# One order replaced by another: h of batches 6 and 7 in 512-token pieces, loads in halves, first q by two queues

## The chip, the cores and the metric

The kernel runs on one core of a Trainium2 chip. The metric is device time in microseconds of one execution, the median of several runs. The engines that matter are PE (TensorE, matmuls and transposes), DVE (VectorE), ACT (ScalarE), POOL (GpSimd, which here issues the casting loads), SP (SyncE, which issues the other transfers) and the core's 16 DMA engines. PE writes to eight PSUM banks, which DVE and ACT empty.

## The reference

```python
def _attn_ref(q, k, v, g_norm) -> np.ndarray:
    kv = np.einsum('bhsd,bhse->bhde', k, v)
    out = np.einsum('bhsd,bhde->bhse', q, kv)
    rms = np.sqrt(np.mean(out * out, axis=-1, keepdims=True) + 1e-06)
    return (out / rms * g_norm).astype(np.float32)

def _moe_ref(x, w_in, conv_w, w_out) -> np.ndarray:
    h = np.maximum(x @ w_in, 0.0)
    ...
    for k in range(K):
        conv_out += conv_w[k][None, None, :] * hp[:, k:k + S, :]
    gate = 1.0 / (1.0 + np.exp(-conv_out))
    return (h * gate @ w_out).astype(np.float32)
```

q, k and v are float32 of (batch 8, heads 8, tokens 576, 64). The attention has no softmax: k and v of a head make a 64 x 64 matrix, q goes through it, and each head's row is normed. The heads of a token then make a row x of 512, and a feed-forward part follows: h of 1024 columns, a convolution over three neighbouring tokens of each column, a sigmoid gate, and the way back to 512.

## The kernel before

Nothing in this kernel is scheduled by a loop. The string `ORDER` lists 773 steps, each a token such as `kv.4.1@0` (step, batch 4, pair of head pairs 1, in PSUM bank 0) or `rea.1.3.0!V` (the engine that does it, V for DVE and A for ACT). A loop at the end of the kernel body runs the step's function for each token, and each engine, SP and POOL too, executes what its steps issue in exactly that order. A step late on an engine makes all behind it on that engine late. The numbers after `@` are slots: a PSUM bank or a buffer, so a step also waits until whoever used that slot last is done with it.

The steps that the change and the prediction speak of:

- `pre` loads q, k and v of head pairs 0 and 1 of batch 0, and all of k, by SyncE as float32 into a staging tile (`stg`, `stg2`; two of four head-pair tiles make one transfer of 576 KB). `ca.x.w` casts one tile of it to bf16, on DVE or ACT.
- `Lq.b.u`, `Lk.b.u`, `Lv.b.u` load half u of a batch by POOL's queue, cast to bf16 on the way (288 KB written). Without u (`Lq.7`) it is the whole batch. q, k and v each have two buffers, so a load waits for the last reader of the batch that had its buffer before. `Li.j` and `Lo.i` load the weights.
- `qt`, `qc` transpose q and copy it from PSUM; `kv`, `kvc` make and copy the 64 x 64 matrices; `ot` multiplies.
- Batches 0 and 1: `sq`, `on`, `nl`, `mz` square, sum, take the reciprocal root and write x. Batches 2 to 7, in the groups of `NORM`: `sq`, `oc` (copy of the output), `ss`, `ln`, `sl`, `sp`, `mu`. x of a batch is complete with its last `mz` or `mu`.
- h of a batch alone: `hm.b.f.u` (two halves u of the contraction, each four matmuls of 288 columns) and `re`, the ReLU that empties it, 576 columns. h of a pair of batches, 1152 columns, for the pairs in `PAIRH`: `ha.p.f.e` (512 columns, e = 0 or 1, four matmuls) and `rea`, and `hb.p.j` (the last 128 columns for four f at once) and `reb`.
- The convolution c (`CONV`: 0 and 1 are batches 0 and 1, 2 is batches 2 and 3 together, 3 is 4 and 5, and 4 and 5 are batches 6 and 7): `ta`, `aa`, `ab` on DVE, the sigmoid `sg` on ACT, and the gate's product `mg` on DVE. One set of 24 DVE steps of each kind, whatever the order.
- `om.p.k.i.j` is the product with w_out for 128 tokens, `ea` copies it to a row buffer, `st` stores it by SyncE. The last tokens, `om.3.6`, are done in two halves of 256 columns.
- `fi`, `fq` and `fo` are fillers, matmuls on a zero tile. They compute nothing. `fi.36.128` is 36 matmuls of 128 columns.
- `sw.k.6` makes the next store wait until the named load has landed.
- `NoSync` dependencies at the end of the kernel body fix each engine's order.

The constants: `HALF` lists the batches whose loads go in halves, `PAIRH` the pairs whose h is made for both batches at once, `STORES2` the stores that go row block by row block.

Of the kernel before, what the change touches and what calls it, by code (L numbers as in the profile page):

```python
# [66 lines left out]
STORES2 = [(0, 0), (0, 3), (0, 2), (0, 1)]  # L67
# [4 lines left out]
pre@0,0,0 Lq.0.1 ca.q.0!V ca.q.1!V fi.36.128@0 fi.3.128@0 qt.0.0@0 qc.0.0!V@0 fi.1.512@2 fi.20.128@2 ct@0 ca.k.1!V  # L72
ca.k.0!A pn Lv.0.1 ca.v.0!V Lq.1.1@1 ca.v.1!A fq.1.512.0@1 fq.1.256.0@1 kv.0.0@1 Li.2 kvc.0.0!A pc fq.2.512.3@3
ot.0.0@6,4 ca.k.2!A sq.0.0@0 Li.0 fi.3.512@1 fi.2.128@1 on.0.0@0 nl.0.0@0 ca.k.3!V fq.2.512.0@2 fq.1.256.0@2 qt.0.1@2
qc.0.1!V@0 sq.0.1@0 mz.0.0@0 fi.1.512@0 fi.3.128@0 on.0.1@0 nl.0.1 fo.1.384.0.1 kv.0.1@2 kvc.0.1!V Lq.1.0 Li.3
fo.1.384.0.1 fq.1.256.1@6 ot.0.1@6,0 sq.0.2@0 mz.0.1 fq.1.512.0@2 qt.1.1@2 Li.1 Lv.1.0@1 fi.2.128@4 on.0.2@4 sq.0.3@7
nl.0.2@0 qc.1.1!V@0 fo.2.384.0.2 on.0.3@2 nl.0.3 Lk.1.0@1 fo.1.384.0.3 hm.0.5.0@4 mz.0.2 Lq.2.0@0 hm.0.4.0@2 mz.0.3
hm.0.1.0@6 hm.0.5.1 re.0.5!A@0 hm.0.4.1 ta.0.5@0 hm.0.1.1 re.0.4!A ta.0.4 qt.1.0@0 hm.0.0.0@2 hm.0.0.1 hm.0.3.0@4
hm.0.3.1 re.0.1!A ta.0.1@1 Lv.1.1 hm.0.6.0@6 qc.1.0!A@1 Lv.2.1@0 re.0.0!A aa.0.2 hm.0.2.0@0 hm.0.2.1 ab.0.2
fq.1.512.0@2 kv.1.0@2 sg.0.4 ta.0.0 re.0.3!V aa.0.0 Lk.1.1 sg.0.5 ab.0.0 kvc.1.0!A hm.0.6.1 re.0.2!A ot.1.0@4,2  # L80
hm.0.7.0@0 mg.0.2 re.0.6!V sg.0.0 Lq.3.1@1 sq.1.1@0 Lq.2.1 hm.0.7.1 ta.0.3@0 re.0.7!V ta.0.2 qt.2.0@6 qc.2.0!V@1
sq.1.0@1 aa.0.1 fo.5.384.1.1 on.1.0@0 sg.0.1 mg.0.0 nl.1.0@0 fo.5.384.1.0 on.1.1@6 nl.1.1 fo.2.384.1.0 kv.1.1@0
kvc.1.1!A fo.1.384.1.1 fq.1.256.2@6 ot.1.1@0,6 mz.1.0 mz.1.1 sq.1.2@0 qt.3.1@4 sq.1.3@1 Lk.2.1@0 qc.3.1!V@0 Lv.2.0
ab.0.1 on.1.2@2 nl.1.2@0 fo.2.384.1.2 on.1.3@4 nl.1.3 Lk.2.0 mz.1.2 fo.1.384.1.3 hm.1.7.0@2 qt.2.1@4 mz.1.3 hm.1.5.0@0
ta.0.6@1 sg.0.2 ta.0.7 hm.1.7.1 hm.1.5.1 sg.0.3 qc.2.1!V@2 re.1.7!A hm.1.1.0@6 hm.1.1.1 hm.1.4.0@4 Lv.3.1@1 re.1.1!A
hm.1.4.1 aa.0.3 mg.0.1 re.1.5!A kv.2.0@6 re.1.4!A Lo.0 hm.1.2.0@0 hm.1.2.1 ab.0.3 sg.0.6 sg.0.7 hm.1.6.0@2 ta.1.5@0
ta.1.4 Lk.3.1@1 kvc.2.0!V hm.1.6.1 Lo.1 ot.2.0@4,6 re.1.2!A re.1.6!A Lq.3.0 oc.2.1@0 kv.2.1@0 kvc.2.1!A Lq.5.0@0
hm.1.3.0@2 aa.1.2 mg.0.3 hm.1.3.1 sq.2.1@0 hm.1.0.0@0 hm.1.0.1 ta.1.7@1 sq.2.0@1 oc.2.0 ab.1.2 sg.1.5 om.0.0.0.0@7
sg.1.4 re.1.3!V ta.1.6 re.1.0!V ot.2.1@5,3 oc.2.3@1 sq.2.3@2 Lq.5.1 kv.3.1@0 om.0.0.0.1@2 aa.1.3 mg.1.2 om.0.0.1.1
Lk.3.0 sq.2.2@3 oc.2.2 kvc.3.1!V ot.3.1@0,3 ta.1.0@0 Lv.3.0 ea.0.0.1!A@0 ab.1.3 ta.1.1 qt.3.0@5 sg.1.7 sg.1.6  # L90
qc.3.0!V@0 oc.3.3@2 aa.1.0 mg.1.3 sq.3.3@4 om.0.1.1.0@2 oc.3.2 ta.1.3@1 om.0.1.0.0 ea.0.1.0!A@1 Lk.5.1@0 Lq.4.1@1
ta.1.2 om.0.1.0.1@6 om.0.0.1.0 ab.1.0 sq.3.2@5 ea.0.0.0!A aa.1.1 ab.1.1 om.0.1.1.1 sg.1.0 qt.5.1@0 qt.5.0@2 kv.3.0@4
qc.5.1!V@1 sg.1.1 ea.0.1.1!V qc.5.0!V@2 kvc.3.0!A Lq.4.0 om.0.2.1.1@7 mg.1.0 sg.1.3 sg.1.2 ot.3.0@0,4 om.0.2.1.0@6
sq.3.1@6 om.0.3.1.1@2 Lv.5.1@0 sq.3.0@7 ss.2@3 ss.3 ln.1@0 mg.1.1 oc.3.1@3 oc.3.0 sl.1@0 om.0.2.0.1 om.0.3.0.1 st.0.0
ea.0.3.1!A@2 kv.5.1@4 qt.4.1@0 Lk.5.0 sp.3.1.1@2 kvc.5.1!V Lk.4.1@1 mu.3.1.1@0 sp.2.0.1@4 mu.2.0.1 om.0.2.0.0
qc.4.1!A@0 sp.3.0.0@0 sp.3.1.0@2 ea.0.2.1!A@0 om.0.3.1.0@7 sp.3.0.1@4 mu.3.0.0 Lv.5.0 sp.2.1.1@0 mu.3.1.0 om.0.3.0.0
mu.3.0.1 sp.2.1.0@2 ea.0.2.0!A sp.2.0.0@4 mu.2.1.1 mu.2.0.0 mu.2.1.0 hb.1.0@6 Lv.4.1@1 fq.1.256.0@0 kv.4.1@0
ea.0.3.0!A kv.5.0@4 reb.1.0!A@1 kvc.5.0!V ot.5.1@6,2 kvc.4.1!A sq.5.2@0 oc.5.2@0 sq.5.3@1 ha.1.3.0@0 rea.1.3.0!V
ha.1.3.1@1 rea.1.3.1!V oc.5.3 ta.2.3@0 Lk.4.0 ot.5.0@6,4 ha.1.2.0@0 Lv.4.0 rea.1.2.0!V ha.1.2.1@3 oc.5.0@1 rea.1.2.1!V
ta.2.2 sq.5.1@2 Lk.7@0 oc.5.1 aa.2.1 ha.1.1.1@1 kv.4.0@4 sq.5.0@3 rea.1.1.1!A ot.4.1@6,2 kvc.4.0!A qt.4.0@0 oc.4.2@2  # L100
sq.4.3@4 qc.4.0!V@0 ab.2.1 oc.4.3 sq.4.2@5 ha.1.1.0@4 rea.1.1.0!A ta.2.1@1 ha.1.0.0@5 rea.1.0.0!A ha.1.0.1@2
ot.4.0@0,3 rea.1.0.1!A ta.2.0 aa.2.0 sq.4.1@6 sq.4.0@7 ha.1.6.0@5 ha.1.5.1@2 ss.4@6 oc.4.1@3 oc.4.0 ss.5 rea.1.5.1!A
ln.2@0 Lq.7@0 qt.7.1@3 qc.7.1!A@0 qt.7.0@0 om.0.4.0@2 sl.2@0 om.0.4.1 ab.2.0 ha.1.5.0@3 Lv.7@0 rea.1.6.0!A sp.5.0.1@4
sp.5.1.1@6 mu.5.0.1@1 qc.7.0!A@1 Lv.6@1 ea.0.4!A@3 sp.4.1.1@0 mu.4.1.1 ha.1.4.0@2 rea.1.5.0!A sg.2.0 hb.1.1@3 Lq.6@1
mu.5.1.1 sp.5.1.0@0 rea.1.4.0!V sp.5.0.0@4 kv.7@6 ha.1.4.1@2 reb.1.1!A kvc.7!A sp.4.0.0@6 mu.5.0.0 mu.5.1.0 sg.2.1
rea.1.4.1!A sp.4.1.0@4 mu.4.0.0 sp.4.0.1@0 mu.4.1.0 ha.1.7.1@3 sg.2.3 mu.4.0.1 sw.q.6 st.0.4 hb.2.1@2 reb.2.1!V@0
sg.2.2 ot.7.0@4,6 mg.2.0 Lk.6@1 ta.2.5@1 rea.1.7.1!A oc.7.1@0 ta.2.4 kv.6@0 ha.1.7.0@2 kvc.6!V sq.7.1@0 ha.2.3.0@3
# [31 lines left out]
def kernel(  # L139
# [11 lines left out]
    nc = tc.nc  # L151
# [18 lines left out]
    T = {}  # L170
# [87 lines left out]
    def pre():  # L258
# [3 lines left out]
        for x in "qkv":  # L262
            nc.sync.dma_start(out=T["stg"][:, "qkv".index(x)], in_=rows(x, 0, 0, 2))
        if FIRST:
# [4 lines left out]
            out=cw_rows[NR - 1:NR, :].rearrange("o (i d) -> o i d", i=2),  # L269
# [440 lines left out]
```

## Time and profile before

| | |
|---|---|
| median of 3 runs (lowest, highest) | 179.21 us (179.1, 179.8) |
| profiled execution | 179.12 us, span 177.3 us |
| PE busy | 170.3 us, 96% of the span |
| DVE busy | 157.0 us, 89% |
| ACT busy | 139.7 us, 79% |
| POOL busy | 34.7 us, 20% |
| DMA | 27.22 MB, 153 GB/s mean |

The span is the time on the core from the first to the last instruction; the profiled execution's own time has 1.8 us around it. Matmuls are pipelined, so one that is shown as 379 ns long may start 216 ns after the one before; the spacing, not the length, adds up. The profile's chain of waits goes back from the last instruction, at each step to what released it.

The profile has DMA rates in 40 equal slices of 4.43 us:

```profile
DMA  5999999999999996999881000005710000043594
GB/s 184 366 201 200 202 206 210 202 206 208 206 207 233 230 206 88 207 210 205 183 301 64 0 2 4 0 3 213 272 49 0 0 0 4 0 172 123 218 379 173
```

The DMA engines are busy from 4.4 us to 66 us without a break. The casting loads read twice the bytes that they write; the rate counts what is written. The issues by kind, with the size of one and the median time from issue to landing in us:

```profile
q_sb<-in_q_dram POOLq DMA_DIRECT2D x11, 288.0 KB, 10.6
v_sb<-in_v_dram POOLq DMA_DIRECT2D x11, 288.0 KB, 10.7
k_sb<-in_k_dram POOLq DMA_DIRECT2D x10, 288.0 KB, 10.8
stg<-in_k_dram SPq DMA_DIRECT2D x2, 576.0 KB, 6.0
stg<-in_q_dram SPq DMA_DIRECT2D x1, 576.0 KB, 3.9
stg<-in_v_dram SPq DMA_DIRECT2D x1, 576.0 KB, 6.3
```

### The profile page before, as it was taken

To read this page: it belongs to the slowest core of one execution; us is meant where nothing else is said; L and a number is where in the kernel's file an instruction comes from. 1 tells how busy PE (TensorE), PEld (TensorE's weight loads), DVE (VectorE), ACT (ScalarE), POOL (GpSimd) and SP (SyncE) were. 2 spreads that over 40 slices of the span, in tenths; PEclk is the share of its full clock that TensorE was granted. 3 is DMA by queue.
4 is the path that set the end of the run, shared out by engine and by line. 5 is a ranking of instruction groups with operands and counts; after the bars stand their busy time and mean duration, and the time that the engine had idled before them with its cause. 6 is when DMAs were issued, how large, how long until landed. Compare 5 with 4: busy or idle time off the path is not lost.

```text
span 177.3 us, 5289 instructions
## 1 busy us (share of the span) xinstructions
PE 170.3 (96%) x2253; PEld 95.4 (54%) x2253; DVE 157.0 (89%) x282; ACT 139.7 (79%) x219; POOL 34.7 (20%) x60
## 2 busy tenths in 40 slices
PE   7999998899999999999999999999999999999992
PEld 7755765576444454444554454444577754444451
DVE  2757699999999796999999999999999999999931
ACT  2366799899999938999999999987795966494720
POOL 6945640851067005500000000000000000000000
PEclk9999999999999999999999999999999999999999
DMA  5999999999999996999881000005710000043594
GB/s 184 366 201 200 202 206 210 202 206 208 206 207 233 230 206 88 207 210 205 183 301 64 0 2 4 0 3 213 272 49 0 0 0 4 0 172 123 218 379 173
DMA packets 21355, 27.22 MB, mean 153 GB/s; under 512 B 1224, under 2 KB 15828, under 8 KB 21332
## 3 DMA queue, kind: packets, MB, share of 16 engines
q0 software_dynamic: 15072, 15.09, 51.5%
q1 hardware_dynamic: 6256, 11.80, 18.0%
q8 instruction: 17, 0.28, 0.6%
q14 instruction: 6, 0.05, 0.1%
q10 hardware_dynamic: 4, 0.00, 0.0%
HBM read 32.52 MB, written 9.44 MB: 237 GB/s over the span
## 4 chain that ended last, share of the span: by engine, by line
PE 66%; DVE 14%; DMA 8%; ACT 7%; issue 2%; POOL 1%; ACTq 0%; DVEq 0%
PE banks L628 28%; PE banks L534 13%; PE banks L547 12%; DMA v_sb<-in_v_dram 6%; PE banks L296 3%; PE banks L441 2%; ACT sq L448 2%; PE banks L393 2%; ACT h L238 2%; DVE xT L518 2%; DMA out_dram<-row 2%; PE banks L418 2%; DVE taps L583 2%; DVE taps L596 2%; DVE taps L584 1%
## 5 line engine op out<-in xcount | busy, mean ns | idle before, releaser
L628 PE MATMUL banks<-w_out_sb,h 128*128 128x512 bf16 x280 | 63.7, 379 | 0.2
L603 ACT ACTIVATE taps<-taps,cw 128x576 bf16<-128x576 bf16 (+1 forms) x48 | 43.6, 946 | 9.9 <-DVE taps L596 9.8
L628 PEld LDWEIGHTS <-h 128*128 128x128 bf16 x280 | 26.5, 98 | 31.5 <-issue 1.6
L238 ACT ACTIVATE h<-banks 128x512 bf16<-128x512 f32 (+1 forms) x51 | 29.8, 658 | 5.7 <-PE banks L534 4.2
L534 PE MATMUL banks<-xT,w_in_sb 128*128 128x288 bf16 x256 | 33.5, 286 | 0.4
L547 PE MATMUL banks<-xT,w_in_sb 128*128 128x512 bf16 x128 | 30.1, 379 | 0.2 <-ACT row L232 0.2
L534 PEld LDWEIGHTS <-w_in_sb 128*128 128x128 bf16 x256 | 24.6, 98 | 8.3 <-issue 1.6
L232 ACT ACTIVATE row<-banks 128x512 f32<-128x512 f32 (+1 forms) x29 | 16.8, 601 | 9.6 <-PE banks L628 5.6
L590 DVE TENSOR_TENSOR taps<-taps 128x1152 bf16<-128x1152 bf16 (+1 forms) x24 | 22.9, 956 | 0.5
L596 DVE TENSOR_TENSOR taps<-taps,h 128x1152 bf16<-128x1152 bf16 (+1 forms) x24 | 22.8, 952 | 0.3
L609 DVE TENSOR_TENSOR h<-h,taps 128x1152 bf16<-128x1152 bf16 (+1 forms) x24 | 22.7, 951 | 0.2 <-ACT taps L603 0.2
L583 DVE TENSOR_SCALAR taps<-h,cw 128x576 bf16<-128x576 bf16 (+1 forms) x48 | 20.3, 423 | 1.7 <-ACT h L238 1.5
L448 ACT ACTIVATE sq<-banks 128x576 bf16<-128x576 f32 x32 | 20.4, 674 | 1.7 <-PE banks L441 1.7
L584 DVE TENSOR_SCALAR taps<-h,cw 128x576 bf16<-128x576 bf16 (+1 forms) x48 | 20.1, 418 | 0.0
L547 PEld LDWEIGHTS <-w_in_sb 128*128 128x128 bf16 x128 | 11.8, 98 | 14.4 <-issue 1.3
L518 DVE SCALAR_TENSOR_TENSOR xT<-o,cw,banks 128x576 bf16<-128x576 f32 x24 | 18.1, 806 | 0.4 <-PE banks L511 0.3
L232 ACT ACTIVATE o<-banks 128x576 f32<-128x576 f32 x24 | 15.9, 678 | 0.0
L240 DVE TENSOR_SCALAR h<-banks 128x576 bf16<-128x576 f32 (+1 forms) x17 | 12.2, 720 | 1.1 <-PE banks L547 1.0
L354 POOL DMA_DIRECT2D k_sb<-in_k_dram x12 | 8.7, 726 | 20.0 <-PE banks L441 9.4
L227 ACT ACT_TABLE_LOAD x8 | 10.3, 1283 | 2.1 <-issue 2.0
L354 POOL DMA_DIRECT2D v_sb<-in_v_dram x13 | 9.4, 724 | 11.2 <-PE banks L324 4.7
L354 POOL DMA_DIRECT2D q_sb<-in_q_dram x13 | 9.6, 738 | 7.5 <-PE banks L418 6.5
(74 smaller groups left out, 149.1 us busy)
## 6 DMA issues: line engine op xcount, KB each, us to landing
out_dram<-row SPq DMA_DIRECT2D x10, 512.0 KB, 2.8
out_dram<-row SPq DMA_DIRECT2D x15, 256.0 KB, 4.1
q_sb<-in_q_dram POOLq DMA_DIRECT2D x11, 288.0 KB, 10.6
v_sb<-in_v_dram POOLq DMA_DIRECT2D x11, 288.0 KB, 10.7
k_sb<-in_k_dram POOLq DMA_DIRECT2D x10, 288.0 KB, 10.8
stg<-in_k_dram SPq DMA_DIRECT2D x2, 576.0 KB, 6.0
k_sb<-in_k_dram POOLq DMA_DIRECT2D x2, 576.0 KB, 10.1
q_sb<-in_q_dram POOLq DMA_DIRECT2D x2, 576.0 KB, 9.9
```

Source lines behind the costliest of these rows:

```text
L232: nc.scalar.activation(to, fr, AX.Copy)
L238: nc.scalar.activation(to, fr, AX.Relu)
L354: loads[x, b] = nc.gpsimd.dma_start(out=qkv(x, b)[:, w0:w0 + n, :], in_=rows(x, b, w0, n))
L448: nc.scalar.activation(by_r(s), natural(T["ot", b, t][:, :S]), AX.Square)
L534: nc.tensor.matmul(ps[:, e, :HS], w_in_sb[:, t, f * P:(f + 1) * P], x[:, t, e * HS:(e + 1) * HS], start=(t == 0), stop=(t == NT - 1))
L547: nc.tensor.matmul(ps, w_in_sb[:, t, f * P:(f + 1) * P], x[:, t, e * 512:(e + 1) * 512], start=(t == 0), stop=(t == NT - 1))
L583: nc.vector.tensor_scalar_mul(tap[:, 0, f % 2, :n, 8:8 + S], h[:, f], cw[:, f:f + 1])
L590: nc.vector.tensor_add(tap[:, 1, :, :n, :S], tap[:, 0, :, :n, 7:7 + S], tap[:, 1, :, :n, 1:1 + S])
L596: nc.vector.tensor_add(y, y, h[:, 2 * j:2 * j + 2])
L603: nc.scalar.activation(y, y, AX.Sigmoid, scale=scale)
L609: nc.vector.tensor_mul(h, h, T["tap", c, j][:, 1, :, :n, :S])
L628: nc.tensor.matmul(ps[:, 0], h[:, f, m * P:(m + 1) * P], w_out_sb[:, f, :], start=first and f == 4 * i, stop=not first and f == 4 * i + 3)
```

## The change

The reference's arithmetic stays as it is. Batches 6 and 7 join the pairs whose h is made for both batches at once: the 64 steps `hm` shrink to 32, and 16 `ha` and 2 `hb` come. Their loads go in halves, so the six whole loads become twelve. The first load of q is two transfers of one head-pair tile each, one issued by SyncE and one by ScalarE, ahead of k's and v's and ahead of ScalarE's transfer of g_norm. `STORES2` loses one store. And the whole order is another: 771 steps, with other slots, other engines for casts, ReLUs and copies, and other fillers.

```diff
-HALF = [0, 1, 2, 3, 4, 5]
+HALF = [0, 1, 2, 3, 4, 5, 6, 7]
...
-PAIRH = [1, 2]
+PAIRH = [1, 2, 3]
...
-STORES2 = [(0, 0), (0, 3), (0, 2), (0, 1)]
+STORES2 = [(0, 3), (0, 1), (0, 2)]
...
-pre@0,0,0 Lq.0.1 ca.q.0!V ca.q.1!V fi.36.128@0 fi.3.128@0 qt.0.0@0 qc.0.0!V@0 fi.1.512@2 fi.20.128@2 ct@0 ca.k.1!V
-ca.k.0!A pn Lv.0.1 ca.v.0!V Lq.1.1@1 ca.v.1!A fq.1.512.0@1 fq.1.256.0@1 kv.0.0@1 Li.2 kvc.0.0!A pc fq.2.512.3@3
-ot.0.0@6,4 ca.k.2!A sq.0.0@0 Li.0 fi.3.512@1 fi.2.128@1 on.0.0@0 nl.0.0@0 ca.k.3!V fq.2.512.0@2 fq.1.256.0@2 qt.0.1@2
-qc.0.1!V@0 sq.0.1@0 mz.0.0@0 fi.1.512@0 fi.3.128@0 on.0.1@0 nl.0.1 fo.1.384.0.1 kv.0.1@2 kvc.0.1!V Lq.1.0 Li.3
-fo.1.384.0.1 fq.1.256.1@6 ot.0.1@6,0 sq.0.2@0 mz.0.1 fq.1.512.0@2 qt.1.1@2 Li.1 Lv.1.0@1 fi.2.128@4 on.0.2@4 sq.0.3@7
-nl.0.2@0 qc.1.1!V@0 fo.2.384.0.2 on.0.3@2 nl.0.3 Lk.1.0@1 fo.1.384.0.3 hm.0.5.0@4 mz.0.2 Lq.2.0@0 hm.0.4.0@2 mz.0.3
...
-ea.0.3.1!A@2 kv.5.1@4 qt.4.1@0 Lk.5.0 sp.3.1.1@2 kvc.5.1!V Lk.4.1@1 mu.3.1.1@0 sp.2.0.1@4 mu.2.0.1 om.0.2.0.0
-qc.4.1!A@0 sp.3.0.0@0 sp.3.1.0@2 ea.0.2.1!A@0 om.0.3.1.0@7 sp.3.0.1@4 mu.3.0.0 Lv.5.0 sp.2.1.1@0 mu.3.1.0 om.0.3.0.0
-mu.3.0.1 sp.2.1.0@2 ea.0.2.0!A sp.2.0.0@4 mu.2.1.1 mu.2.0.0 mu.2.1.0 hb.1.0@6 Lv.4.1@1 fq.1.256.0@0 kv.4.1@0
...
-sp.6.1.0@4 sp.7.1.1@6 om.1.1.1.0 mu.6.1.0 mu.7.0.0 ha.2.4.1@0 hm.6.0.0@4 hm.6.0.1 ab.3.1 mu.7.1.1 hm.6.1.0@2 sg.3.1
...
-om.3.1.1.0 om.3.0.1.1 ea.3.1.0!V sg.5.1 ea.3.0.1!V sg.5.3 mg.5.1 st.3.1 om.3.3.1@2 om.3.4.1@0 sg.5.0 st.3.0 om.3.2.1@1
-mg.5.0 ea.2.0.1!V st.2.0 om.3.4.0 ea.3.4!A@1 om.3.2.0 om.3.5.0 ea.3.2!V@3 om.3.3.0 st.3.4 st.3.2 ea.3.5!A@2 st.3.5
-ea.3.3!V@0 st.3.3 om.3.6.1@0 ea.3.6.1!V@1 st.3.6.1 om.3.6.0 ea.3.6.0!A@3 st.3.6.0
+pre@0,0,0 Lq.0.1 ca.q.0!A ca.q.1!V fi.32.128@0 fi.1.128@0 qt.0.0@0 ca.k.0!A ca.k.1!A ca.v.1!V ca.v.0!A qc.0.0!V@0
+ca.k.3!V Lv.0.1 Li.2 fi.4.128@2 fi.28.128@2 ct@7 pc Lq.1.1@1 fq.1.256.0@2 kv.0.0@2 kvc.0.0!A fq.1.512.1@4 fq.1.256.1@4
+ot.0.0@0,2 sq.0.1@0 fi.3.512@4 fi.2.128@4 on.0.1@4 sq.0.0@7 nl.0.1@0 pn mz.0.1@0 ca.k.2!A fi.2.512@6 on.0.0@6 Li.0
+nl.0.0 Lq.1.0 qt.0.1@4 fo.3.384.0.0 fq.1.512.0@2 kv.0.1@2 qc.0.1!V@0 mz.0.0 kvc.0.1!A fq.2.512.1@6 ot.0.1@6,4 sq.0.2@0
+sq.0.3@1 fi.3.512@0 fi.2.128@0 on.0.2@0 nl.0.2@0 fi.1.512@2 on.0.3@2 nl.0.3 mz.0.2 fo.2.384.0.3 hm.0.4.0@0 mz.0.3
+qt.1.1@2 qc.1.1!V@0 Li.1 hm.0.5.0@6 hm.0.5.1 re.0.5!A@0 ta.0.5@0 hm.0.4.1 re.0.4!A Lv.1.0@1 qt.1.0@2 hm.0.1.0@4
+hm.0.1.1 hm.0.0.0@0 qc.1.0!A@1 hm.0.0.1 Lk.1.0@1 hm.0.3.0@2 ta.0.4 aa.0.2 hm.0.2.0@6 hm.0.2.1 re.0.1!A ab.0.2 re.0.0!V
...
+om.0.1.1.0 om.0.0.0.0@3 ea.0.1.0!A oc.3.3 om.0.0.1.0 kv.3.0@0 qt.5.1@4 aa.1.1 ab.1.1 sg.1.0 qt.5.0@6 om.0.2.1.1@2
+qc.5.1!V@1 sg.1.1 kvc.3.0!A ot.3.0@0,4 Lk.4.1@1 ea.0.0.0!V qc.5.0!V@2 sg.1.2 sg.1.3 om.0.2.1.0@3 om.0.3.1.1@6 mg.1.0
+ss.2@7 mg.1.1 Lv.4.0@1 sq.3.0@6 sq.3.1@7 ss.3 ln.1@0 sl.1@0 om.0.3.0.1 om.0.2.0.1 oc.3.0@3 oc.3.1 ea.0.3.1!A@2
+kv.5.1@0 Lk.5.0 kvc.5.1!V Lv.4.1 qt.4.1@4 qc.4.1!A@0 sp.2.0.1@6 sp.3.1.1@0 om.0.2.0.0 sp.3.1.0@4 mu.2.0.1@0
...
+st.1.0 om.1.1.0.1@6 om.1.1.1.1 ha.3.0.1@1 ha.3.6.1@2 ta.3.3 ha.3.6.0@3 om.1.1.0.0 ea.1.1.0!A@1 ha.3.5.0@4 aa.3.1
+ab.3.1 mg.3.3 rea.3.6.0!A@1 ta.3.5@1 ea.1.1.1!A sg.3.2 ha.3.7.1@5 ea.1.4!A@2 rea.3.7.1!A ha.3.7.0@3 ha.3.2.0@7
+rea.3.2.0!A st.1.4 sg.3.3 ha.3.4.0@6 ha.3.3.1@0 ha.3.3.0@5 rea.3.6.1!A rea.3.3.0!A rea.3.4.0!A ha.3.2.1@7 rea.3.2.1!A
...
+ea.3.1.0!A sg.5.3 st.3.1 mg.5.1 ea.3.0.1!V st.3.0 sg.5.1 sg.5.0 mg.5.0 om.3.5.0 om.3.3.0 ea.3.5!A@1 ea.3.3!A@3
+om.3.4.0 ea.3.4!A@0 st.3.5 st.3.3 st.3.4 om.3.2.0 om.3.6.0@0 ea.3.2!A@2 st.3.2 ea.3.6.0!V@1 st.3.6.0 om.3.6.1
+ea.3.6.1!A@3 st.3.6.1
...
         for x in "qkv":
             qkv(x, 0)
         T["stg"] = work.tile([P, 3, 2, S], FP32, name="stg", tag="h1", bufs=1)
-        for x in "qkv":
+        for w, queue in enumerate((nc.sync, nc.scalar)):
+            queue.dma_start(out=T["stg"][:, 0, w:w + 1], in_=rows("q", 0, w, 1))
+        for x in "kv":
             nc.sync.dma_start(out=T["stg"][:, "qkv".index(x)], in_=rows(x, 0, 0, 2))
         if FIRST:
             T["stg2"] = work.tile([P, len(FIRST), 2, S], FP32, name="stg2", tag="h0", bufs=1)
```

## The prediction

> **What bounds the kernel now.** I read the page's busy shares first, then the table of busy time by stage, then the chain of work that ended last, then what VectorE waited for. The stage table (windows of the span, busy us per engine, then clock, DMA share, GB/s):
>
> ```profile
> core 0: us, PE busy (x) PEld busy (x) DVE busy (x) ACT busy (x) POOL busy (x), PEclk, DMA share, GB/s
> 0.00:20.00 20.00, 18.28 (x359) 13.10 (x359) 11.51 (x37) 9.81 (x16) 13.04 (x30) 1.00 1.09 233
> 20.00:60.00 40.00, 38.70 (x748) 22.95 (x739) 38.53 (x78) 38.73 (x64) 17.23 (x24) 1.00 1.21 212
> 60.00:90.00 30.00, 29.53 (x618) 15.54 (x605) 27.69 (x43) 26.17 (x43) 4.47 (x6) 1.00 1.04 183
> 90.00:170.00 80.00, 79.98 (x574) 41.47 (x561) 77.51 (x125) 63.78 (x98) 0.00 (x0) 1.00 0.23 84
> ```
>
> No engine is free. From 20 to 60 us PE, DVE and ACT are each 96 to 97% busy, and after 90 us PE and DVE still are (79.98 and 77.51 of 80). PE's figure hides fillers: matmuls on zeros (`fi`, `fq`, `fo`) that only fill waits, some 8.7 us of them after the first warming block. DVE has none, so its idle time is the honest measure of slack:
>
> ```profile
> engine line waited for: us in total, times, longest us
> DVE taps L583 <- ACT h L238: 1.5, 1, 1.5
> DVE hi L499 <- ACT rs L492: 1.4, 2, 1.2
> DVE h L240 <- PE banks L547: 1.0, 1, 1.0
> DVE kvw L234 <- PE banks L393: 0.4, 1, 0.4
> ```
>
> These are DVE's waits from 18 to 170 us, nearly all there are. The last two sit at 66 to 68 us, behind one transfer that the chain shows (start, us, what):
>
> ```profile
> 54.24 0.72 POOL k_sb L354
> 54.95 0.08 issue
> 55.03 0.71 POOL v_sb L354
> 55.74 10.40 DMA v_sb<-in_v_dram
> 66.14 0.04 issue
> 66.19 0.82 PE banks L393 x72
> ...
> 142.68 26.85 PE banks L628 x124
> 169.53 0.03 ACTq L232
> ```
>
> `Lv.4.1`, v of batch 4, lands at 66.14, and `kv.4.1` waits for it. The end is PE alone: 124 matmuls in a row, 0.2165 us each. But DVE is no further off: its last gating multiply `mg.5.0` ends at 168.26 (two from 166.83, 1.43 us), and `om.3.4.0`, which needs it, ends with its copy's start at 169.60, so it began 4 x 0.2165 earlier, at about 168.7. DVE's slack at the end is 0.4 us.
>
> **How I price the change.** I walked both order texts and priced each step at the spacing of its instructions in the chain: 0.28 us for a one-batch tap multiply, 0.68 and 1.355 for the one- and two-batch adds, 0.77 for `mz` and `mu`, 0.72 and 0.68 for a ReLU on DVE, 0.69 for a row copy there, 0.46 for a cast, 0.2157 for a 512-column matmul, 0.1248 for 288 columns, 0.058 for 128. For before this gives DVE 156.7 us against the page's 157.05.
>
> **Part 1, h of batches 6 and 7.** 128 matmuls of 288 columns (15.97 us in the chain) become 64 of 512 (64 x 0.2157 = 13.80) and 32 of 128 (32 x 0.058 = 1.86): -0.3 us of PE. The 16 ReLUs (12 on ACT, 4 on DVE) become 18 (16 ACT, 2 DVE): ACT +2.9 (16 x 0.668 - 12 x 0.646), DVE -1.6 (4 x 0.75 - 2 x 0.686). ACT was 64 of 80 us busy after 90, so its share is hidden; were ACT full there it would cost 2.9.
>
> **Part 2, DVE and ACT anew.** The search moves other work too: DVE gets 12 ReLUs in batches 2 to 5 instead of 8 (+2.8), and 4 row copies instead of 8 (-2.8); the casts of q's pair 0 and k's pair 1 go to ACT, v's two change places (-0.9). The total falls from 156.7 to 154.2, but *where* it falls matters. Split at `mz.0.3` (x of batch 0 complete) and at `mg.5.0`: before 9.8 / 144.4 / 2.5, after 7.9 / 145.9 / 0.4. The first part is no gain: DVE was idle 8.5 of the first 20 us. The last is behind the final matmuls. In between DVE has **1.5 us more** than before, chiefly `qc.1.1` pushed behind `mz.0.3` (0.68), one more small `kvc` (0.28) and the balance of ReLUs and copies. ACT too has 0.9 us more between `nl.0.3` and `ln.1`, where it was full.
>
> **Part 3, the first loads.** Before, q of pairs 0 and 1 is one SyncE transfer, issued at 0.74 (0.43 us) and landed at 4.62; DVE casts twice, `qt.0.0` runs at 5.54. Now two halves go out on two queues, ACT and DVE cast side by side (0.68 instead of 0.86) and 33 cold fillers instead of 39 stand ahead (6 x 0.111 = 0.67 us). On ACT the added issue stands ahead of g_norm's and of the table load (1.96 to 3.24); 0.43 later that still ends before q lands. How much sooner q lands no row shows. Lower end: not sooner, since the DMA engines move 366 GB/s in the next slice and 590 KB at that rate is 1.6 us in any case. Upper end: half of the 1.6, 0.8. I take 0.2, half the old issue.
>
> The Trainium skill, "DMA: Bandwidth & Descriptors", section "Issuing engines are not separate DMA queues", speaks against this part: transfers started by different engines share the same 16 DMA engines, and starting them together saves only sequencer time. By it q gains at most the 0.2 and the sum below stands; without it q gains up to 0.8 and x of batch 0 the 0.4 that is its bound below, so the sum would be 0.2 less. No row of before has one tensor on two queues.
>
> Whatever q gains meets two later arrivals. v's first half lands at 8.06. Its casts still share ACT and DVE, but the first matmul of `kv.0.0` now needs ACT's: 8.06 + 0.68 = 8.74 instead of 8.52; the second needed ACT's before too. `qc.0.0` (0.75), done at 7.05 before, is queued on DVE behind v's cast and ends at 9.3, when `ot.0.0` still waits for `kvc.0.0` (started at 9.65). So these cost nothing, and `ot.0.0` gains nothing. And `kv.0.1` starts at 13.14 because `Lv.0.1` has just landed. It waits its turn behind all 2.36 MB of staged inputs, whose bytes don't change. So x of batch 0 comes 0 to 0.4 us sooner; I take **0.2**.
>
> **Part 4, loads in halves.** Six more issues of 0.73 us on POOL, busy 20% and idle beside its own queue: nothing, 4.4 us if it were full. Bytes are equal. Order counts: at the 200 GB/s of the slices from 9 to 40 us a half (295 KB written) takes 1.47 us. `Lv.4.1` had 29 loads of q, k and v ahead, now 28 (`Lv.5.0` and `Lq.4.0` go behind it, `Lv.4.0` ahead): it lands about 1.5 us sooner, and the 1.4 us of DVE waits at 66 to 68 go, **if the queue doesn't run dry**. What stands behind `Lk.4.1`'s wait for `kv.3.0` (released at 54.24) is now `Lv.4.0`, `Lk.5.0`, `Lv.4.1`: fourth instead of third. The quickest landing of a half in the trace, 6.0 us, gives 54.2 + 6.0 + 3 x 1.47 = 64.6; the median, 10.8, gives 69.4. I take the first, because two fewer loads are queued ahead of the wait. Later loads have more room: `kv.6` moves some 10 us of PE work back.
>
> **Part 5, fillers and tail.** Fillers after the first block grow from 8.7 to 9.4 us, in waits that stay. The tail, PE's end at 173.86 to 177.3, keeps its form: `ea.3.6` waits for an earlier store to leave its row buffer. The 512 KB store that ran just ahead now goes out earlier: -0.2, bounds 0 and -0.4 (the last copy started 0.4 after PE).
>
> **Sum.** From `mz.0.3`'s end (16.52 + 1.54 = 18.06) to `mg.5.0`'s end, 150.2 us passed for 144.4 of DVE work: 5.8 lost. After: 145.9 + (5.8 - 1.4) = 150.3. With -0.2 ahead and -0.2 in the tail: **-0.3 us**. PE checks it: from the first `hm` on it has 0.3 us more (fillers up, h down) and loses about 0.9 less at 60 to 66, -0.6 without DVE; the later of the two decides. The profiled execution took 179.12 us, span 177.3 and 1.8 around it, 0.1 under the median 179.21. Forecast 178.8.
>
> **Rivals.**
> - *The new order packs better.* Only the two waits that no order removes stay, the first ReLU (1.5) and the norm chain (1.4): 145.9 + 2.9 = 148.8, 1.4 sooner, with 0.4 from start and tail 177.3. For it: PE lost 7.3 us between first `hm` and last matmul, which a tighter order could recover, and `Lk.1.0` stands one load sooner. Against: with three engines at 97% a late step delays all. Chance 0.34.
> - *Slower: the load of batch 4 stays late.* If POOL's wait at `Lk.4.1` lets the queue run dry, `Lv.4.1` lands no sooner than 66.14 and DVE still loses 5.8: 145.9 + 5.8 is 1.5 over, less 0.2 in the tail, and the start's 0.2 gone: 180.4; with the median landing, 69.4, about 181 or more. It decides as soon as DVE loses over 4.3 us after x of batch 0. For it: ACT and DVE both carry more in the full stage. Chance 0.28.
> - *The two transfers do nothing for q.* The fillers are then followed by a wait and 0.2 is lost: 179.0, inside the forecast's case.
>
> **How the numbers follow.** What this kernel's measurement can tell from no change is about 0.5%, 0.9 us. The forecast's case holds 0.38 (its own range 178.3 to 179.6, no change), packing 0.34 (faster), the late load 0.28 (slower). The range reaches 177.0 to 180.9: below by the first rival less the start's upper end, above by the second.
>
> **What would show it.** Right: `Lv.4.1` landing near 64.7, DVE idle from 18 to 170 us near 4, `kv.0.0` at about 8.8, `kv.0.1` still ruled by its load at 13, h of batches 6 and 7 in about 15.7 us of PE. Wrong: `mg.5.0` ending before 167.3 or after 169.2; q's cast starting before 4.0; a new PE gap at `kv.4.1`.

## The result, and the profile after

| | before | after |
|---|---|---|
| median (lowest, highest) | 179.16 us (179.09, 179.8; 4 runs) | 184.99 us (184.48, 186.96; 4 runs) |
| ratio, 95% interval | | 1.0338 (1.0305 to 1.0371) |
| profiled execution, its span | 179.12, 177.3 us | 186.96, 185.2 us |
| PE's end, last multiply's end | 173.86, 168.26 us | 182.08, 176.66 us |

The changed kernel is 5.8 us slower than the one before, outside the predicted range. Its profiled execution is the slowest of its four, by 1.6 us; what sets it apart comes with the clock below. Lines of the code move by +3 (L550 is L547 of before), in the kernels below with one q transfer by +1, those of the helpers by +1.

The same four stages of the changed kernel (busy us of PE, PEld, DVE, ACT, POOL, then clock, DMA share, GB/s):

```profile
0.00:20.00 20.00, 17.01 (x272) 11.45 (x273) 7.78 (x31) 10.11 (x16) 11.48 (x28) 0.91 1.08 232
20.00:60.00 40.00, 38.84 (x751) 23.96 (x751) 38.66 (x77) 37.83 (x61) 17.21 (x24) 1.00 1.18 192
60.00:90.00 30.00, 26.36 (x472) 13.36 (x470) 23.07 (x37) 21.62 (x37) 10.02 (x15) 0.94 1.14 200
90.00:170.00 80.00, 79.72 (x677) 37.66 (x676) 78.13 (x123) 67.06 (x104) 0.00 (x0) 1.00 0.22 75
```

Two stages are new. From 60 to 90 us PE is busy 26.36 us and was 29.53, DVE 23.07 and was 27.69: all engines lost time together there. In the first and third stage the granted clock, third figure from the end, is below 1.00. What DVE waited for from 18 to 170 us:

```profile
DVE hi L502 <- ACT rs L495: 4.0, 2, 2.6
DVE xT L473 <- ACT o L466: 2.4, 1, 2.4
DVE h L241 <- PE banks L550: 1.5, 2, 1.3
DVE xT L521 <- PE banks L514: 1.4, 2, 1.1
```

The first grew from 1.4 to 4.0 us; the second ends at 19.33 us and belongs to the late start of this execution; the third, 1.0 before, was forecast to go and is still there. Where the 60 to 90 us stage stalls, the chain of the changed kernel says (start, us, what):

```profile
70.16 5.10 DMA k_sb<-in_k_dram
...
75.35 0.36 SPq L653
...
75.75 0.46 SPq L653
...
76.26 0.62 SPq L653
...
76.92 8.43 DMA out_dram<-row
...
85.46 0.61 ACT row L233
...
86.11 1.86 PE banks L550 x4
```

This reads from top to bottom. `Lk.7.1` lands at 75.26. SyncE had been held at `sw.k.7` for it; now it issues the stores `st.0.3` and `st.0.1` one after another among the loads, and the last one needs 8.43 us. Only then is row buffer 0 free, and ACT's copy `ea.0.4` is next for that buffer. PE needs the copy's PSUM bank. PE's own list of waits has it in one line, and a second one that is new:

```profile
PE banks L550 <- ACT row L233: 3.4, 1, 3.4
PE banks L396 <- ACT v_sb L233: 1.6, 1, 1.6
```

In the kernel before, `ea.0.4!A@3` took a buffer that no other row of this pair had used; here all four rows went to `ea.0.1@0`, `ea.0.0@1`, `ea.0.3@2` and `ea.0.2@3`, and `ea.0.4!A@0` waits for a store. ACT held at `ea.0.4` is also late with the reciprocal root behind it, which gives DVE's 2.6 us at L502.

Behind each long stand of PE the clock falls. Windows of the changed kernel, early and at the stall:

```profile
9.00:10.00 1.00, 0.00 (x0) 0.00 (x0) 0.54 (x2) 0.54 (x1) 1.00 (x2) 1.00 1.21 225
...
11.00:12.00 1.00, 1.00 (x13) 0.37 (x10) 0.90 (x5) 0.16 (x2) 0.00 (x0) 0.50 1.26 190
12.00:13.00 1.00, 1.00 (x3) 0.30 (x2) 0.90 (x7) 1.00 (x2) 0.40 (x1) 0.50 1.39 198
```

```profile
84.00:86.00 2.00, 0.00 (x0) 0.00 (x0) 0.00 (x0) 0.54 (x2) 0.00 (x0) 0.89 1.21 211
86.00:88.00 2.00, 1.89 (x7) 0.78 (x7) 1.41 (x4) 1.47 (x3) 0.00 (x0) 0.50 1.21 207
```

Within 86 to 90 us at clocks of 0.50 and 0.76 PE loses another 2 x 0.50 + 2 x 0.24 = 1.5 us of work. The fall at 11 us is this execution's own: its mean granted clock is 0.980, that of the other three 0.991. v landed at 9.46 in it (8.06 before, 7.6 to 8.5 in the profiled runs of the kernels below), so `kv.0.0` ran at 10.20. The end of the chain:

```profile
174.64 0.75 DVE h L612
175.39 0.60 DVE row L235
175.99 0.68 DVE h L612
176.66 0.05 issue
176.71 3.63 PE banks L631 x16
180.34 1.76 PE banks L624 x16
```

The last multiply gates `om.3.5.0`: PE's last matmuls wait for DVE here, where PE alone was the end before.

### The profile page after: what moved, and what is told of

Its sections match the earlier page's. It is cut to its first block, busy times and chain, and to the rows that moved or that the text cites. A ratio compares the mean times of both kernels' runs of the same rounds, so it can differ in the third digit from the quotient of the medians.

```text
span 185.2 us, 5239 instructions
## 1 busy us (share of the span) xinstructions
PE 173.8 (94%) x2225; PEld 92.2 (50%) x2225; DVE 154.7 (84%) x278; ACT 143.3 (77%) x227; POOL 38.7 (21%) x66
## 4 chain that ended last, share of the span: by engine, by line
PE 33%; DVE 32%; DMA 15%; ACT 10%; issue 6%; SPq 1%; POOL 1%; DVEq 0%; ACTq 0%; POOLq 0%
PE banks L550 11%; PE banks L631 7%; DMA k_sb<-in_k_dram 7%; DVE taps L593 6%; DVE taps L599 6%; DVE h L612 5%; DMA out_dram<-row 5%; DMA stg<-in_v_dram 4%; DVE xT L521 4%; DVE taps L587 4%; DVE taps L586 4%; ACT taps L606 2%; ACT h L239 2%; PE banks L565 2%; PE banks L396 2%
## 5 line engine op out<-in xcount | busy, mean ns | idle before, releaser
L550 PE MATMUL banks<-xT,w_in_sb 128*128 128x512 bf16 x192 | 45.0, 384 | 3.4 <-ACT row L233 3.4
L233 ACT ACTIVATE row<-banks 128x512 f32<-128x512 f32 (+1 forms) x33 | 18.7, 592 | 15.5 <-PE banks L631 6.9
L550 PEld LDWEIGHTS <-w_in_sb 128*128 128x128 bf16 x192 | 18.2, 98 | 24.9 <-issue 4.9
L537 PE MATMUL banks<-xT,w_in_sb 128*128 128x288 bf16 x128 | 17.4, 286 | 0.1
L233 ACT ACTIVATE o<-banks 128x576 f32<-128x576 f32 x24 | 15.6, 675 | 0.9 <-PE banks L444 0.8
L357 POOL DMA_DIRECT2D k_sb<-in_k_dram x14 | 10.1, 720 | 24.9 <-PE banks L396 20.1
L241 DVE TENSOR_SCALAR h<-banks 128x512 bf16<-128x512 f32 (+1 forms) x19 | 13.1, 702 | 1.5 <-PE banks L550 1.5
L537 PEld LDWEIGHTS <-w_in_sb 128*128 128x128 bf16 x128 | 12.0, 98 | 4.3 <-issue 1.0
L357 POOL DMA_DIRECT2D q_sb<-in_q_dram x15 | 10.7, 715 | 15.6 <-PE banks L421 13.6
L299 PE MATMUL banks<-zero 128*128 128x128 bf16 (+1 forms) x81 | 10.3, 303 | 1.3 <-DVE zero L281 1.3
```

Of the source, the lines that this page charges most:

```text
L233: nc.scalar.activation(to, fr, AX.Copy)
L537: nc.tensor.matmul(ps[:, e, :HS], w_in_sb[:, t, f * P:(f + 1) * P], x[:, t, e * HS:(e + 1) * HS], start=(t == 0), stop=(t == NT - 1))
L550: nc.tensor.matmul(ps, w_in_sb[:, t, f * P:(f + 1) * P], x[:, t, e * 512:(e + 1) * 512], start=(t == 0), stop=(t == NT - 1))
```

## The experiments

Theory: the hold `sw.k.7`, through the row buffer, costs some 4 us, and the rest is VectorE's 1.5 us more. Rivals: the start (two transfers, late v), the wider pieces of h, the loads in halves, a PE order that is simply worse.

**e1_no_hold.** In the changed order:

```diff
-oc.5.0 sw.k.7 st.0.3 rea.1.1.0!A st.0.1 rea.1.2.1!V
+oc.5.0 st.0.3 rea.1.1.0!A st.0.1 rea.1.2.1!V
```

> The changed kernel with one token gone: the stores of rows 384 to 639 and 128 to 383 of the first pair (st.0.3, st.0.1) no longer wait for the load Lk.7.1. Theory hold: in the changed kernel ea.0.4 waits on ACT for the landing of st.0.1 (85.46, idle 3.5 us) and PE stands for 3.4 us, so without the hold 3 to 4 us go: about 181.3, and the PE gap at ea.0.4 and the second fall of the granted clock are gone. Theory order (the new order is simply less well balanced, DVE decides from 88 us on): the stall only fills time that DVE needs anyhow, at most 1 us goes: 184 or more. The start stays as it is in both.

Measured: 181.03 us (180.28 to 181.94), 1.0097 of before (1.0063 to 1.0131). One token is worth 4.0 of the 5.8 us. PE's 3.4 us wait for ACT's row is gone; its wait for v is 1.1 us in this profile, and the clock stayed at 1.00 behind it.

**e2_one_q.** The changed kernel with the first q as before:

```diff
-        for w, queue in enumerate((nc.sync, nc.scalar)):
-            queue.dma_start(out=T["stg"][:, 0, w:w + 1], in_=rows("q", 0, w, 1))
-        for x in "kv":
+        for x in "qkv":
```

> The changed kernel with the first q again as one SyncE transfer, all else as changed. Theory two queues: v's staged tiles land at 8.1 again instead of 9.5, PE doesn't idle 1.6 us before kv.0.0, the granted clock stays 1.0 at 10 to 14 us, and 1 to 3 us go: 182 to 184. Theory POOL order (the casting loads, reordered, take the DMA engines earlier) or theory fillers (PE stands because 32 fillers are too few): v still lands near 9.5 or PE idles all the same, and the time is 184.5 to 186.

Measured: 184.79 us (183.69 to 185.89), 1.0295 (1.0242 to 1.0349): 0.2 below the changed kernel, inside the interval. In its profile v lands at 8.23, PE stands 1.0 us for it and the clock stays at 1.00 until 14 us; the stall at ACT's row is still there, 2.9 us. In no profile but the changed kernel's, with two transfers or with one, did v land later than 8.5, so its 9.46 is hardly the two transfers' doing.

**e3_both**, both edits together:

> Both edits: no hold on st.0.3 and st.0.1, and one transfer for q. If the two causes add: 179 to 181, the rest being DVE, which has 1.5 us more between x of batch 0 and its last multiply. If only one of them matters, it equals that one alone (181.3 or 182 to 184).

Measured: 180.59 us (180.34 to 181.54), 1.0073 (1.0049 to 1.0096). The hold, measured a second time, is 184.79 - 180.59 = 4.2 us. What is left over before is 1.3 us.

**e4_before_split**, the two q transfers alone, in the kernel before (e2's edit the other way round):

> The kernel before with nothing changed but the first q in two transfers, by SyncE and ScalarE. Theory two queues: v lands about 1.4 us later than 8.06 here too, kv.0.0 waits, the time is 180 to 182. Theory POOL order or fillers: v lands at 8.1 and the time stays at 179.2, within 0.4.

Measured: 179.78 us (179.39 to 180.57), 1.003 (1.0012 to 1.0048): 0.5 us slower, between the two expectations. In two transfers q's tiles land at 4.21 to 4.61 us (five profiles; 4.31 here), in one transfer at 4.45 to 4.69 (eleven profiles): some 0.2 us sooner in the mean. But in this profile v lands at 8.32 instead of 8.06, `kv.0.1` runs at 13.96 instead of 13.14, and the first matmul of h is 0.8 us later than before. The split brings nothing and costs a little; which of the loads it delays was not pursued.

**e8_st01_first** keeps the hold and the two transfers, and takes only the store of row buffer 0 out of its reach:

```diff
-oc.5.0 sw.k.7 st.0.3 rea.1.1.0!A st.0.1 rea.1.2.1!V
+oc.5.0 st.0.1 sw.k.7 st.0.3 rea.1.1.0!A rea.1.2.1!V
```

> The changed kernel with st.0.1 put ahead of the hold: it goes out as soon as its rows are copied, and only st.0.3 still waits for Lk.7.1. Theory row buffer (ea.0.4 takes the buffer of st.0.1, so the hold stops ACT through that buffer): the 4 us go as without any hold, about 181. Theory traffic (the held stores, sent among the loads of batches 6 and 7, make everything late): st.0.3 still goes out at 75 us among the loads, so most of the loss stays, 184 or more.

Measured: 180.51 us (179.57 to 182.63), 1.0057 (1.003 to 1.0083), as low as without any hold. So it is the row buffer, not the hold as such. PE's longest waits in this kernel:

```profile
PE banks L299 <- DVE zero L281: 1.3, 1, 1.3
PE banks L396 <- ACT v_sb L233: 0.6, 1, 0.6
PE banks L631 <- issue: 0.3, 2, 0.2
```

The line for ACT's row (3.4 us) is absent, and nothing has taken its place. Its clock is 1.00 behind the 0.6 us wait.

**e7_before_halves**, the six whole loads of batches 6 and 7 in halves, in the kernel before (`HALF` and the six tokens: `Lk.7@0` becomes `Lk.7.0@0 Lk.7.1`, and so on):

> The kernel before with the six whole loads of batches 6 and 7 as twelve halves in the same places of POOL's order. Theory nothing: bytes and order are equal, 179.3 within 0.4. Rival (each issue of 0.73 us and each piece's own latency push the loads of batch 6 past their use at 84 to 90 us): 180 or more.

Measured: 179.42 us (178.93 to 180.08), 1.0008 (0.9994 to 1.0021). Nothing, as forecast.

**e6_before_wide**, h of batches 6 and 7 in 512-token pieces, in the kernel before; each `hm`/`re` becomes an `ha`/`rea` in its place:

```diff
-PAIRH = [1, 2]
+PAIRH = [1, 2, 3]
...
-mu.7.0.0 ha.2.4.1@0 hm.6.0.0@4 hm.6.0.1 ab.3.1 mu.7.1.1 hm.6.1.0@2 sg.3.1
+mu.7.0.0 ha.2.4.1@0 ha.3.7.0@4 ab.3.1 mu.7.1.1 ha.3.7.1@2 sg.3.1 mg.3.0
...
+st.1.0 ha.3.5.0@0 hb.3.1@1 hb.3.0@5 sg.4.6 aa.4.1 om.2.2.0.0@4 mg.4.3 ab.4.1 rea.3.4.0!A reb.3.1!A reb.3.0!A sg.4.2
```

> The kernel before with h of batches 6 and 7 alone in 512-token pieces: each pair of half-contraction steps is replaced in place by one piece of four matmuls, the two remainders of 128 columns come at the end, the engines of the ReLUs stay and the two added ones go to ACT. Theory: PE 0.3 us less, DVE's four ReLUs a little shorter, ACT 1.5 to 2 us more where it has room: 178.7 to 179.2. Rival (the pieces cover both batches, so the first gates of batch 6 wait for twice the matmuls, and DVE starves): 180 or more.

Measured: 180.69 us (179.91 to 181.07), 1.006 (1.0025 to 1.0096): 1.4 us slower, though by the price of its matmuls PE has 0.3 us less work. The wait that holds most of the loss, and the window of this kernel around it:

```profile
PE banks L547 <- DVE xT L518: 1.1, 1, 1.1
```

```profile
120.00:130.00 10.00, 8.82 (x51) 3.60 (x49) 10.00 (x14) 7.50 (x9) 0.00 (x0) 1.00 0.63 236
```

DVE (third figure after the length) is full here, as it was before in the same window; PE, which was full too, now stands 1.1 us for DVE's x: a piece of 512 tokens needs x of *both* batches, where `hm.6` began with x of batch 6 alone. So the slower outcome came, by another wait than its rival had named. In place, the pieces cost time; the changed order has `om` steps there instead.

**e5_relu_act.** In e3's kernel four ReLUs go from VectorE to ScalarE (`rea.2.6.1`, `rea.2.1.1`, `rea.3.1.0`, `rea.3.5.1`: `!V` becomes `!A`):

> The kernel without the hold and with one q transfer (180.59), and four late ReLUs (f 6 and 1 of batches 4 and 5, f 1 and 5 of batches 6 and 7) moved from DVE to ACT: DVE 2.7 us less, ACT 2.4 more. Theory DVE (what is left of the loss is DVE's 1.5 us more up to its last multiply): the last multiply ends 1.0 to 1.5 us sooner and the time is 179.1 to 179.6. Theory PE (the new order's waits and fillers on PE): no change, 180.4 to 180.8. Theory ACT (its 3.7 us more decide): slower, 181 or more.

Measured: 181.29 us (180.95 to 181.83), 1.0114 (1.009 to 1.0138), slower. The window of this kernel:

```profile
100.00:110.00 10.00, 8.60 (x149) 4.28 (x149) 8.91 (x13) 10.00 (x17) 0.00 (x0) 1.00 0.01 3
```

and of e3:

```profile
100.00:110.00 10.00, 10.00 (x163) 4.71 (x160) 9.90 (x16) 10.00 (x17) 0.00 (x0) 1.00 0.01 2
```

ACT was full at 100 to 110 us already. The two ReLUs of batches 4 and 5 fell into that stage, and PE and DVE now wait beside it. The run says nothing of VectorE's late work; the next two put the ReLUs where ACT has room.

**e9_late_relu_act** moves only `rea.3.1.0` and `rea.3.5.1`; **e10_late_rows_act** two row copies as well (the diff shows these):

```diff
-ab.5.0 ea.2.1.1!V st.2.1
-ea.3.1.0!A sg.5.3 st.3.1 mg.5.1 ea.3.0.1!V st.3.0 sg.5.1 sg.5.0 mg.5.0
+ab.5.0 ea.2.1.1!A st.2.1
+ea.3.1.0!A sg.5.3 st.3.1 mg.5.1 sg.5.1 sg.5.0 ea.3.0.1!A st.3.0 mg.5.0
```

> The changed kernel without its store hold and with q in one transfer (180.6 us), with two ReLUs late in the order, rea.3.1.0 and rea.3.5.1, moved from VectorE to ScalarE, behind the stage from 100 to 110 us in which ScalarE is full; nothing else is changed. Theory VectorE-late: what is left of the loss over before (about 1.3 us) is VectorE's work, which gates the last multiply; 1.4 us less of it brings the end 0.5 to 1.0 us forward, to 179.6 to 180.2 us, and the last multiply from 170.0 to about 169.2. Rival PE-and-ScalarE: what is left is PE's order and ScalarE's 2.9 us more; then 180.6 us or more, with the last multiply at 170 or later.

> As the run with the two late ReLUs on ScalarE, and two row copies, ea.2.1.1 and ea.3.0.1, from VectorE to ScalarE too (the second one behind sg.5.0, so that ScalarE makes the last gates first): another 1.4 us less on VectorE, right before the last multiply mg.5.0. Theory VectorE-late: 178.8 to 179.5 us, with the last multiply at about 168.5. Rival PE-and-ScalarE: no gain over the run before it, or a loss of up to 0.7 us, since ScalarE takes two copies of 0.6 to 0.8 us among the last gates.

Measured: 180.34 us (179.95 to 180.73), 1.006 (1.0037 to 1.0083), and 180.47 us (179.93 to 181.12), 1.0059 (1.0032 to 1.0085). VectorE lost 1.4 and then 2.8 us of work, and the time fell by 0.25 us, within the intervals, and no further. In e9 the last multiply ends at 169.48, 0.5 us sooner, near the theory's 169.2, but the time lies between the two expectations: at most 0.25 of the 1.3 us is VectorE's late work. e10 is no clean second step, since its last two multiplies wait 0.25 and 0.57 us for ScalarE's gates, as its rival had it. The chain of e9 shows why the multiply's half microsecond is not in the time:

```profile
142.22 1.05 PE banks L563 x16
...
150.21 23.31 PE banks L629 x108
173.52 1.76 PE banks L622 x16
```

With a little less on DVE, PE is without a gap from 142 us to its end at 175.28, 1.4 later than before's 173.86. In e3 PE had waited 0.21 us for the last multiply; that gap is about all that relieving DVE could bring.

**e11_all**, e10 with e8's order of stores:

> As the run with the late ReLUs and row copies on ScalarE, with the store hold kept, but st.0.1 sent ahead of it, so that only st.0.3 is held and the row buffer of ea.0.4 comes free early. If the hold costs by the row buffer alone, the hold that is left spares the load queue two stores and the time is 0.1 us below the run without any hold (180.5 against 180.6 where this was tried alone): 178.7 to 179.4 us. If the hold also costs by the stores' own wait, 0.5 us or more above it.

Measured: 180.41 us (180.2 to 181.06), 1.0067 (1.0043 to 1.0091). That is outside its range of 178.7 to 179.4 and within 0.1 us of e10: with `st.0.1` ahead, the hold that is left costs nothing, and nothing is gained.

**e12_before_relu_act**, the control: `re.6.5!V` and `re.7.4!V` of the kernel before become `!A`.

> Control: the kernel before with two ReLUs of h, re.6.5 and re.7.4, from VectorE to ScalarE, nothing else. If VectorE gated the kernel before as tightly as the changed one, 1.4 us less of its work gives 178.3 to 178.8 us. If before stood by PE's order with VectorE a little behind, it stays within 0.4 us of 179.3.

Measured: 178.77 us (178.66 to 179.07), 0.9976 (0.9954 to 0.9999). It lies at the upper edge of the first expectation's range, 0.13 us from the second's: 0.4 us faster than before (179.16 beside it), the only kernel here that beats it, by an interval that just leaves 1. It does not decide between the two. PE's end moved only from 173.86 to 173.74; the rest of its shorter span, 176.9 for 177.3, is tail.

**e13_mu_first.** PE's idle time was the next suspect. By the PE rows of its windows e9 idles more than before in two places; before:

```profile
0.00:10.00 10.00, 8.42 (x149) 1.00 0.84 267
...
80.00:90.00 10.00, 9.70 (x215) 1.00 0.95 186
```

and e9:

```profile
0.00:10.00 10.00, 7.70 (x153) 1.00 0.85 269
...
80.00:90.00 10.00, 9.16 (x131) 1.00 0.96 172
```

That is 0.7 and 0.5 us. The first costs nothing, because the first matmul of h, which waits for x of batch 0, begins at the same time in both, before and e9 in this order:

```profile
16.54 3.24 PE L534 MATMUL banks<-xT,w_in_sb 128*128 128x288 bf16 x24
16.53 0.65 PE L535 MATMUL banks<-xT,w_in_sb 128*128 128x288 bf16 x4
```

Before, more fillers stood in that wait. The second is a wait of 0.7 us in two for DVE's multiplies `mu.4`, in front of which `ab.2.0` stands. e13 is e9 with

```diff
-ab.2.0 sp.4.0.1@0 reb.1.1!A rea.1.4.1!A mu.4.0.1@1
+sp.4.0.1@0 reb.1.1!A rea.1.4.1!A mu.4.0.1@1
...
-sp.5.0.1@0 mu.4.0.0 mu.4.1.1 Lv.7.0
+sp.5.0.1@0 mu.4.0.0 mu.4.1.1 ab.2.0 Lv.7.0
```

and **e14_mu_first_split** the same with e8's start and stores.

> The kernel with the two late ReLUs on ScalarE (no store hold, q in one transfer; 180.3 us) with one addition of VectorE, ab.2.0 (1.35 us), moved behind the first four multiplies that make x of batches 4 and 5, in front of which it stands now. In its trace TensorE stands 0.84 us at 82 to 86 us for those multiplies and is full from 145 us to the end. Theory TensorE-idle: what is left of the loss is TensorE's idle time, 0.84 us of it here against 0.35 us in the kernel before, so the stand goes and the time falls by 0.3 to 0.8 us, to 179.5 to 180.0 us. Rival, that the idle time here is made good later (VectorE or ScalarE sets the pace from 100 to 140 us): 180.2 to 180.5 us, with the stand gone in the trace but TensorE's end where it was, and a new wait between.

> The changed kernel with its two first q transfers kept, the hold kept for st.0.3 alone (st.0.1 sent ahead of it), the two late ReLUs on ScalarE and ab.2.0 behind the first multiplies. TensorE-idle theory: the 0.45 us that TensorE waits for q in the kernels with one transfer is absent, but that wait lies before v, for which it then waits longer, so nothing is gained by it: within 0.3 us of the run with ab.2.0 moved and q in one transfer. If q's two transfers cost 0.2 to 0.5 us as they did in the kernel before and in the changed one, it lies that much above it; if the wait for q counts, 0.4 us below.

Measured: 180.78 us (180.53 to 181.06), 1.0088 (1.0071 to 1.0105), and 180.72 us (180.11 to 181.22), 1.0077 (1.0059 to 1.0095). No gain, rather a small loss. The wait was not removed but moved; e13's PE list has

```profile
PE banks L548 <- DVE h L241: 0.6, 1, 0.6
...
PE banks L512 <- DVE xT L519: 0.2, 1, 0.2
```

0.6 us for a ReLU now queued behind `ab.2.0`, for 0.7 us at L512 in e9. And e14, with the two transfers of q and the hold on `st.0.3`, does not differ from e13.

## Why the prediction was wrong

**The step that failed is the sum: it has no term for the store hold.** The walk over the new order priced every engine's work and the loads, and passed over `sw.k.7`, which is queued on SyncE ahead of `st.0.3` and `st.0.1`, and over the slot of `ea.0.4!A@0`, which waits for `st.0.1`. Both tokens were in the text. What is late behind them: ACT's copy at 85.46, ACT's reciprocal root of batches 4 and 5, DVE's multiplies, PE. Removing the hold gave 4.0 and 4.2 us, and moving one store ahead of it 4.5. None of the rivals had this wait; the slower one put its loss on a load, at the wrong place.

In the sum's own terms, from x of batch 0 to the last multiply, with DVE's work as the trace has it: before 150.2 us, 143.6 of them work and 6.6 lost (the sum's 144.4 and 5.8 use the walk's prices). The forecast was 150.3, with 1.5 us more work and 1.4 less lost. The changed kernel took 155.8, with 145.6 of work and 10.2 lost. Without the hold and with one q transfer (e3) it is 152.2, with 145.7 of work and 6.5 lost. So beside the hold two terms of the sum failed: the credit of 1.4 us came out as 0.1, and the work grew by 2.1 instead of 1.5.

**Part 4, first half right, second wrong.** Loads in halves cost nothing (179.42 against 179.31 for before beside it). The landing was forecast well: in e3 `Lv.4.1`, issued at 55.87, lands 7.9 us later, at 63.8, where 64.6 was forecast and 66.14 was before. But the credit of 1.4 us for it failed. In e3 `kv.4.1` runs at 66.15, at 66.19 before, because `hb.1.0` stands ahead of it in PE's order and ends at 66.15. Before, `hb.1.0` ended at about 65.8, so even there the load held PE for 0.4 us at most; the prediction read a wait behind a chain's transfer as wholly that transfer's. Of DVE's two waits there, the 0.4 us for `kv.4.1` went and the 1.0 us for the ReLU became 1.5; e3's longest are

```profile
DVE h L241 <- PE banks L548: 1.5, 2, 1.3
DVE hi L500 <- ACT rs L493: 1.2, 1, 1.2
```

and all waits of this list add up to 4.8 us, 5.0 before. Whether the queue ran dry, the condition written beside the credit, does not matter then; in e3 the rate falls from 206 GB/s at 52 to 54 us to 142 at 58 to 60, with the DMA engines still busy.

**Part 2, direction right, size and price wrong.** DVE's work between x of batch 0 and the last multiply grew as said, by 2.1 us instead of 1.5; 0.8 of it are three slow tap multiplies (below). In e3 that multiply ends at 169.99, 1.7 later than before, beyond the 169.2 given as a sign of being wrong. But DVE's work does not go into the time one for one. 1.4 us less of it late in the order gave 0.25 us and 2.8 us gave no more (e9, e10), since PE is full right behind it. The check by PE, -0.6 us, had the wrong sign: without the hold and with DVE relieved (e9), PE takes 158.75 us from the first matmul of h to its end and took 157.32 before. It stands 2.6 us in that time instead of 1.8, where 0.9 us less was forecast, and its fillers there are 5.1 us instead of 4.5.

**Part 1** had the work right: 0.216 us for a 512-column matmul and 0.056 to 0.066 for a 128-column one give 15.6 to 15.9 us, for 15.66 forecast. What it left out is that a wide piece needs x of both batches; in the old order that is a wait of 1.1 us, in a kernel 1.4 us slower (e6).

**Part 3.** q came 0.2 us sooner, as taken, and nothing followed; the split cost 0.5 us in the kernel before and 0.2 and 0.4 in the changed one (e2 against it, e3 against e1), the last two inside the intervals. The Trainium skill's rule ("DMA: Bandwidth & Descriptors", section "Issuing engines are not separate DMA queues"), by which only sequencer time is saved, agrees with the 0.2 us. `kv.0.0`, forecast at 8.8, ran at 8.37 to 9.05 in e1, e8 and e14, whose start is the changed kernel's, and at 10.20 in its own profile with v late. `kv.0.1`, forecast at 13 and ruled by its load, ran at 12.80 to 13.36 in those three and at 15.79 in its own profile. The first matmul of h ran at 16.33 to 16.91 in the three, 16.54 before: x of batch 0 was not sooner.

**Part 5.** From PE's end to the end of the span it is 3.1 us and was 3.4: 0.3 shorter, where 0.2 was forecast.

**What stays open** is why the last 1.1 to 1.3 us are spent. Where they lie can be said: e9's PE ends 1.4 us later than before, all of it behind the first matmul of h; 0.6 us are stands from 60 to 90 us, 0.4 stands after that, 0.6 more filler work in front of waits before 60 us, and 0.2 us of stands are saved there. The stand that was attacked, at 82 to 86 us, turned into another, and no run took the fillers' waits away. That this is the price of the new order as a whole, with three engines nearly full, fits all runs but was only argued.

## What to carry to other kernels

When an order is written out by hand, follow the buffers as well as the engines: for each copy into a shared buffer, name the store that must leave it first, and everything that this store is held behind. A hold that keeps stores out of the way of loads is free only while a buffer is left over; here the same hold cost 4 us or nothing, by whether one of two stores stood behind it or ahead of it. Where two engines end close together, work taken from one of them is worth the gap between them, not its own duration: 1.4 us of it gave 0.25 here, with a gap of 0.21. And a wait that ends with a transfer costs only what the engine would not have waited anyhow: look at what else stands in front of the step before crediting an earlier landing.

## What the runs showed of the hardware

- A stand of PE can cost more than itself. After 1.58 us (changed kernel) the granted clock was 0.50 for some 3 us, and after the 3.4 us stall again, as after one of 2.9 us in e2; after 1.13 us (e1) and 0.6 us (e8) it stayed at 1.00. The stall's real price is therefore 3.4 + 1.5 us of PE, of which some was made good. The Trainium skill ("TensorE: Matmul & The Clock Gate", section "Why this matters for your kernels") warns of PE gaps above about 3 us; half of that was enough once here, and where the two differ the run decides.
- The four 256 KB stores that the hold released among the casting loads took 7.2 us in the median to land, the last one 8.43; the median of all stores of that size in the same run is 2.6. Without the hold (e1) they went out earlier, also among casting loads, and took 6.7.
- The landing of the first v differs from profile to profile by 1.8 us (7.6 to 9.5) among kernels whose loads up to it are the same bytes. In the one where it came at 9.46, the first matmul of h ran at 19.35, 2.4 us later than in e1.
- Three tap multiplies of 1152 columns just ahead of the normalisation of batches 4 and 5 took 0.72 to 0.80 us instead of 0.50 in most kernels of the changed order, only the first two of them in e14, and only the first in e8 and e13. POOL was issuing loads beside them; where the third or the second stayed short, POOL's last two issues took 1.57 to 1.72 us instead of 1.43 to 1.47. But POOL was also issuing beside such multiplies in e7, where they took 0.52 and its issue no longer than others. It is 0.8 us of DVE. The Trainium skill ("GPSIMD Engine Reference", section "Specifications") says that VectorE and GpSimd share their SBUF interfaces and that VectorE's two-port modes can contend there; e9 and e7 together show that this alone doesn't settle it, and the cause is open.
